# A banded attention with a three-way maximum feed-forward: one written-out order of work replaced by another

## The chip, the cores and the metric

The kernel runs on one core of a Trainium2 chip. The core has a matrix engine (TensorE, in the profile PE, with its weight loads as PEld), a vector engine (VectorE, DVE), a scalar engine (ScalarE, ACT), a general one (GpSimd, POOL) and a sync engine (SyncE, SP), which here issues nearly all transfers (DMAs). They run side by side and wait for each other by semaphores. Matmul results go to PSUM, 8 banks of 512 fp32 columns for 128 partitions; everything else lies in SBUF.

The metric is the device time of one execution in microseconds. The kernel before takes 175.69 us (median of 3 runs, 175.66 to 176.38).

## The reference

```
q, k, v: [4, 8, 768, 64] fp32          # batch, heads, positions, width
scores = q k^T / 8                     # per batch and head
keep   = (key < 8) or (0 <= query - key < 96)
bias   = -slope[head] * dist           # dist = query - key inside the band, 96 for a global key outside it
a      = softmax(where(keep, scores + bias, -1e9))
x      = (a v), heads side by side: [3072, 512]
h      = max(x w1, x w2, x w3)         # [3072, 768]
out    = h w_out                       # [3072, 512] fp32
```

## The kernel before, in words

The 3072 rows are 24 tiles of 128, six per batch. A query tile sees its own key tile and the one before it. The 8 global keys of a batch are kept from its first tile and copied over rows of later tiles that are no longer needed, so that "the tile before" also brings the global keys. Softmax needs no maximum: exp, a product with a mask that holds exp(bias) (or a bias that PE adds to the scores beforehand), a column of ones in v for the row sums, and a division at the end.

The feed-forward works on 7 chunks of 4, 2, 2, 4, 4, 4 and 4 tiles (`SIZES`). For each chunk c and each of 6 blocks f of the 768 columns, three groups of four matmuls (j = 0, 1, 2 for w1, w2, w3) go to three banks; the first is copied out, the second and third are merged by maxima.

Nothing is scheduled by a compiler. `SCHEDULE` is a string of some 780 units, and each engine works through its instructions in the order of the string. A unit may end in `@slot`, the place in a ring of buffers (`RINGS`) or the first PSUM bank that it takes, and a last digit may say which engine does it (0 ACT, 1 DVE, 2 POOL). T is a tile, G a pair of tiles, g a half of the heads, a is 0 for q, 1 for k, 2 for v.

| unit | work | line |
|---|---|---|
| l a.G.p | load q, k or v of a pair; p = 2 all heads, 0 or 1 a half. G = 12 loads q or k of the first four tiles, where p = 2, 3 are quarters | L229, L236 |
| c a.G.p.e | cast q or k to bf16; on POOL in two halves | L195, L201 |
| x, y | transpose on PE, copy out of PSUM | L270, L276; L283, L287 |
| X T | transposing DMA of a tile's q and k in place of x and y | L292 |
| v T.e.w | cast half of a tile's v | L254 |
| G T.w, V T.e.w | copies of the global keys, and of the global values | L313, L315; L323, L325 |
| B, K, R | bias rows, mask rows, their base | L373, L378, L561 to L565 |
| b, S T.g | bias by PE into the scores' bank; scores | L335, L349 |
| e T.g, m T.g | exp on ACT; product with the mask (left out where b was used) | L356; L365, L367 |
| A T, n T | attention product; division by the row sums | L391, L394; L402, L403 |
| t, u | x transposed by PE and copied out (ACT or DVE) | L418, L421 |
| Z T | x transposed by a DMA instead | L424 |
| w, W; q, Q | load and cast w1 to w3; load and cast w_out | L514, L195, L201; L523 |
| F c.f.j | four matmuls of the feed-forward | L433 |
| f c.f.j.w | j = 0: copy out (ACT or DVE); j = 1, 2: maximum (DVE) | L447; L449, L452 |
| O, o, s | output matmuls of a tile, copy out, store | L457, L471, L477 |
| E | output of the last chunk, with banks and staging slots from `LAST_BANKS` and `LAST_STAGES` | L457, L462, L463 |
| D n.w | n matmuls of w columns of zeros, which nothing reads | L532 |

In the body, the string is all that sets the order (the setup stands between the second and the third unit):

```
for u in todo[:2] + [None] + todo[2:]:
    ...
    code, _, slot = u.partition("@")
    units[code[0]](int(slot) if slot else None, *(int(n) for n in code[1:].split(".") if n))
```

Two rings matter below. PSUM's 8 banks are shared: a feed-forward group or an output takes one, scores and attention products take two, and a unit can start only when the unit that emptied its bank is done. Transfers of SP's queue are issued strictly in order, each behind its own waits: for its buffer, for the data it reads, and, after the first eight, for the landing of an earlier one.

Of the kernel before, what the change touches and what calls it, by code (L numbers as in the profile page):

```python
# [34 lines left out]
    F0.2.0@5 f0.4.0.1@1 F0.1.0@6 v4.1.2 v4.0.2 l2.3.2@0 f0.1.0.0@2 q2@0 v5.1.0 F0.0.0@0 F0.5.1@1 F0.4.1@4  # L35
    F0.2.1@6 m4.0.1 f0.0.0.0@3 v5.0.0 f0.5.0.0@4 m5.1.1 A4@2 V4.1.0 F0.3.1@0 W0.1.2 f0.4.1.1 W0.2.0 m5.0.1
    f0.5.1.1 F0.0.1@1 F0.1.1@4 V4.0.1 W1.2.0 n4@1 t4@7 A5@2 W2.2.0 c1.3.2.2@0 f0.0.1.1 f0.1.1.1 F0.1.2@1
    n5@0 u4.1@1 f0.1.2.1@0 F0.0.2@4 q0@1 t5@7 u5.0 q1@2 f0.3.1.1 f0.0.2.1 F0.2.2@2 F0.3.2@3 f0.3.2.1
    c0.3.2.0 f0.2.0.0@2 f0.2.1.1 F1.2.0@4 F1.0.2@7 Q2.0 v7.1.2 F1.0.0@5 f1.0.0.1@3 v6.1.2 F1.0.1@3 f0.2.2.1
    f1.0.1.1 f1.2.0.1@0 Q0.2 f1.0.2.1@1 x3.1.2@6 y3.1.2.1@3 F0.4.2@5 f0.4.2.1 l1.4.2@3 v6.0.2 Q1.2 F1.1.0@0  # L40
    F1.2.2@1 l0.4.2@4 l1.6.2@5 F1.2.1@4 f1.2.1.1 F1.3.1@2 f1.2.2.1 F1.3.2@3 v7.0.2 F1.3.0@4 f1.3.0.0@2
    f1.3.1.1 f1.3.2.1 x3.0.2@1 F0.5.2@5 f0.5.2.1 F1.4.0@2 F1.1.1@3 f1.1.0.0@3 y3.0.2.0 S6.0.0@0 S6.1.0@4
    G6.2 c1.4.2.2@1 c0.4.2.2 l0.5.2@0 c0.5.2.2@2 f1.1.1.1 f1.4.0.0@1 e6.0@4 S7.0.0@6 S7.1.0@2 l1.5.2@6
    c1.5.2.2 e6.1@5 c1.6.2.2@0 e7.1@6 F1.4.1@0 e7.0@7 l2.4.2@1 O0.2@1 f1.4.1.1 m7.1.1 x4.1.2@0 F1.5.2@2
    F1.5.0@3 m7.0.1 v8.1.2 F1.5.1@4 A7@6 f1.5.0.1@0 m6.1.1 m6.0.1 o0.2.0@0 y4.1.2.0@0 f1.5.1.1 f1.5.2.1
    x4.0.2@3 y4.0.2.0 G7.0 l0.6.2@1 c0.6.2.2 F1.4.2@5 O0.1@4 f1.4.2.1 n7@2 o0.1.1@1 A6@0 l2.5.2@2 S8.1.0@2
    S8.0.0@6 n6@3 V7.1.1 G8.1 v8.0.2 F1.1.2@4 O0.3@5 t6@0 v11.0.2 v9.0.2 v9.1.2 f1.1.2.1 V7.0.0 t7@1 e8.1@0
    e8.0@3 S9.0.0@2 u6.0@2 S9.1.0@6 m8.1.1 u7.1 o0.3.0@2 O0.0@4 e9.1@1 m8.0.1 o0.0.0@3 e9.0@2 F2.4.0@5
    m9.1.1 f2.4.0.0@2 A8@0 V8.0.2 n8@1 F2.5.0@4 F2.2.1@6 f2.5.0.1@4 F2.1.0@7 f2.1.0.0@0 G9.0 F2.5.1@5 V8.1.2
    F2.2.0@4 f2.5.1.1 m9.0.1 f2.2.0.0@1 X10@1 X11 S10.1.0@0 f2.2.1.1 e10.1@6 S10.0.0@2 e10.0@7 v10.0.1 X12@2  # L50
    G10.1 G12.1 F2.4.1@7 A9@4 V9.1.2 V9.0.2 X13 O1.0@6 l2.7.2@0 n9@0 S12.0.0@0 f2.4.1.1 m10.0.1 l2.6.2@1
    v10.1.1 e12.0@4 S11.1.0@2 S11.0.0@4 e11.1@5 F2.2.2@7 f2.2.2.1@0 F2.3.0@0 F2.1.1@1 F2.0.0@7 f2.3.0.0@3
    m10.1.1 e11.0@0 f2.0.0.0@1 A10@2 V10.0.2 f2.1.1.1 m11.1.1 o1.0.0@4 n10@3 Z8@0 V10.1.0 l0.7.2@2 v11.1.2
    v15.1.2 v12.1.2 F2.5.2@0 O1.1@1 v12.0.2 S12.1.0@2 e12.1@3 S13.1.0@4 m11.0.1 Z9 f2.5.2.1 S13.0.0@6
    o1.1.1@5 F2.4.2@0 A11@2 n11@2 F2.0.1@1 e13.1@1 F2.3.1@4 m12.0.1 m12.1.1 e13.0@2 c0.7.2.1@1 Z10 f2.0.1.1
    m13.1.1 F2.0.2@5 f2.3.1.1 t11@2 F2.1.2@3 l0.9.2@3 l1.8.2@4 u11.0 G13.0 f2.1.2.1 f2.0.2.1 F2.3.2@6
    F3.4.0@2 F3.0.0@1 f3.4.0.0@4 f3.0.0.1@0 m13.0.1 v13.1.1 f2.4.2.1 F3.1.0@4 F3.3.0@5 c0.9.2.0@2 f3.3.0.0@1
    A12@2 n12@1 f2.3.2.1 f3.1.0.1@2 F3.1.1@1 f3.1.1.1 v13.0.1 l1.9.2@0 c1.9.2.1 F3.0.2@0 F3.0.1@5 f3.0.1.1
    F3.1.2@4 f3.0.2.1@1 F3.2.0@1 F3.2.2@2 l1.7.2@6 c1.7.2.2 f3.1.2.1 F3.5.0@3 A13@4 V13.1.1 f3.5.0.1@3 n13@0
    l2.9.2@2 l0.8.2@5 c0.8.2.2@0 v19.0.2 V13.0.0 f3.2.0.0@0 v14.0.2 F3.5.1@0 l2.8.2@1 F3.2.1@6 f3.2.1.1  # L60
    f3.2.2.1 F3.3.1@1 F3.5.2@3 v18.1.0 X14@3 v14.1.2 X15 f3.5.1.1 f3.3.1.1 F3.4.1@2 c1.8.2.0 S14.0.0@4
    S14.1.0@0 e14.0@6 G14.2 f3.4.1.1 F3.4.2@6 f3.5.2.1 F3.3.2@7 e14.1@7 f3.4.2.1 m14.0.1 m14.1.1 v19.1.2
    v15.0.2 S15.0.0@0 e15.0@0 S15.1.0@2 G15.1 e15.1@5 f3.3.2.1 O2.0@6 A14@0 V14.1.2 o2.0.1@6 n14@3 X18@0
    O2.1@7 v18.0.0 o2.1.0@7 m15.0.1 S18.0.0@0 S18.1.0@2 X19 Z13@1 V14.0.1 O3.3@6 m15.1.1 e18.0@3 e18.1@4
    X16@1 o3.3.0@8 A15@0 n15@2 O3.0@7 S19.1.0@0 v17.1.1 m18.0.1 S16.1.0@2 m18.1.1 e19.1@1 S16.0.0@4 O3.2@6
    o3.0.1@9 e16.0@2 V15.1.2 A18@0 e16.1@6 n18@0 o3.2.1@10 m16.1.1 X17 O3.1@7 G16.0 Z14 o3.1.0@11 m16.0.1
    V15.0.1 S17.0.0@0 v16.0.0 Z12 S19.0.0@2 Z15 e19.0@7 S17.1.0@4 e17.1@0 m17.1.1 F4.4.0@6 e17.0@5 l0.11.2@1
    s1.0 l2.10.2@0 F4.2.0@7 l1.10.2@2 F4.1.0@2 F4.5.0@3 v16.1.0 F4.3.0@0 A16@4 f4.2.0.0@2 Z18@2 V16.1.2
    f4.3.0.0@0 v20.0.2 G18.0 F4.1.2@1 f4.1.0.1@3 c0.11.2.2@1 m17.0.1 v17.0.1 l2.11.2@2 n16@3 s3.1 f4.5.0.0@4
    V16.0.2 m19.0.1 l0.10.2@3 F4.0.1@0 F4.1.1@7 m19.1.1 f4.4.0.0@1 F4.5.2@6 c0.10.2.2@2 A19@2 Z16 n19@1 Z19  # L70
    G19.0 s0.1 V19.0.2 s2.1 f4.1.1.1 f4.1.2.1@0 V19.1.1 F4.0.0@4 F4.4.1@5 A17@2 c1.10.2.0 f4.0.0.1@3 n17@2
    F4.5.1@7 f4.5.1.1 F4.2.1@1 F4.3.2@4 f4.5.2.1 f4.4.1.1 F4.0.2@2 F4.3.1@3 F4.4.2@5 f4.2.1.1 v22.1.1
    f4.0.1.1 f4.3.1.1 f4.0.2.1 f4.3.2.1 F4.2.2@1 Z17 F5.1.1@0 F5.2.0@3 F5.5.0@2 s1.1 F5.3.0@4 F5.0.0@6
    f4.2.2.1 f5.3.0.0@4 f5.0.0.0@3 v21.1.2 F5.1.0@1 s0.0 l1.11.2@0 F5.3.1@4 c1.11.2.2 f5.2.0.1@0 f4.4.2.1
# [537 lines left out]
```

## Time and profile before

| | |
|---|---|
| median of 3 runs | 175.69 us (175.66 to 176.38) |
| the profiled execution | 176.69 us, of which the span of the trace is 174.8 us |
| TensorE clock granted | 0.996 of full speed |
| transfers | 37.36 MB, mean 214 GB/s |

The page gives busy times of the engines, the chain of work that ended last, and the costliest groups of instructions with a mean in ns and the idle time in front of them. Other views are the windows (busy time of each engine in a stretch, in the order PE, PEld, DVE, ACT, POOL, each with its count of instructions, then the granted clock, the share of the DMA engines that is busy, and GB/s), the chain in order of time (start, length, what), and the timeline (start, length, engine, line, operation, out<-in, count, and in brackets the idle time before it and what ended it). In the groups by form, the two numbers behind the bar are the busy time in us and the mean of one in ns.

### The profile page before, as it was taken

What the parts mean: (1) busy time and instruction counts of PE and PEld (TensorE: products, weight loads), DVE (VectorE), ACT (ScalarE), POOL (GpSimd) and SP (SyncE); (2) the same over time, 40 slices, a digit from 0 to 9 for tenths busy, and PEclk for the clock granted to TensorE, in tenths of its full rate; (3) what the DMA queues carried; (4) which work ended last, traced back from release to release, by engine and by line L of the source; (5) the groups of instructions that cost most, each with busy time, mean ns of one, the idle gap of its engine ahead of it and who ended that gap; (6) DMA issues with size and microseconds to landing.
All of it is one profiled execution on the core that took longest, in us unless ns stands there. A gap on an engine that the chain in (4) does not pass through costs nothing.

```text
span 174.8 us, 3865 instructions
## 1 busy us (share of the span) xinstructions
PE 165.9 (95%) x1485; PEld 93.6 (54%) x1507; DVE 131.9 (75%) x268; ACT 95.4 (55%) x147; POOL 54.7 (31%) x99
## 2 busy tenths in 40 slices
...
GB/s 149 352 292 327 402 360 385 270 371 311 229 303 179 139 183 266 267 290 284 165 135 112 114 145 306 305 210 260 231 213 20 0 120 137 121 286 4 0 119 185
DMA packets 66403, 37.36 MB, mean 214 GB/s; under 512 B 24144, under 2 KB 61392, under 8 KB 66384
## 3 DMA queue, kind: packets, MB, share of 16 engines
...
q8 instruction: 12, 0.20, 0.5%
q10 hardware_dynamic: 144, 0.07, 0.1%
...
## 4 chain that ended last, share of the span: by engine, by line
PE 76%; DVE 10%; DMA 6%; ACT 3%; issue 2%; SPq 0%; DVEq 0%
PE psum L433 44%; PE psum L457 17%; PE psum L349 6%; DMA xT<-xb 3%; DMA rawqk<-in_k_dram 3%; DVE P L365 3%; PE psum L391 3%; PE psum L394 2%; PE psum L276 2%; DVE ht L452 1%; DVE xb L403 1%; ACT P L356 1%; PE psum L270 1%; DVE qb L195 1%; PE psum L335 1%
## 5 line engine op out<-in xcount | busy, mean ns | idle before, releaser
L433 PE MATMUL psum<-xT,w 128*128 128x512 bf16 (+1 forms) x491 | 97.5, 348 | 1.5 <-DMA xT<-xb 0.7
L433 PEld LDWEIGHTS <-w 128*128 128x128 bf16 x504 | 47.6, 98 | 42.9 <-DMA xT<-xb 0.9
L356 ACT ACTIVATE P<-psum 128x1024 bf16<-128x1024 f32 (+1 forms) x48 | 43.3, 954 | 10.4 <-PE psum L349 10.3
L449 DVE TENSOR_TENSOR h<-h,psum 128x512 bf16<-128x512 bf16 (+1 forms) x42 | 25.0, 605 | 15.9 <-PE psum L433 12.4
L457 PE MATMUL psum<-wo,ht 128*128 128x512 bf16 (+2 forms) x147 | 33.4, 362 | 0.5
L447 ACT CAST h<-psum 128x512 bf16<-128x512 f32 (+1 forms) x27 | 13.8, 523 | 33.1 <-PE psum L433 29.8
L452 DVE TENSOR_TENSOR ht<-h,psum 128x512 bf16<-128x512 bf16 (+1 forms) x42 | 26.2, 644 | 2.1 <-PE psum L433 0.9
L365 DVE TENSOR_TENSOR P<-P,wmask 128x1024 bf16<-128x1024 bf16 x34 | 25.2, 752 | 2.0 <-ACT P L356 1.7
L457 PEld LDWEIGHTS <-ht 128*128 128x128 bf16 x156 | 13.8, 98 | 13.5 <-DVE ht L452 0.2
L254 POOL CAST va<-rawv 64x512 bf16<-64x512 f32 x28 | 18.5, 668 | 4.8 <-DMA rawv<-in_v_dram 3.7
L323 POOL COPY va<-vaf 4x260 int32<-4x260 int32 x17 | 7.2, 424 | 34.9 <-PE psum L394 34.5
L403 DVE TENSOR_TENSOR xb<-psum,rz 128x512 bf16<-128x512 f32 x24 | 16.6, 692 | 0.8
L201 POOL CAST qb<-rawk 128x512 bf16<-128x512 f32 x12 | 7.5, 654 | 23.7 <-DMA rawk<-in_k_dram 23.7
L349 PE MATMUL psum<-qkT 64*128 64x128 bf16 x352 | 14.4, 217 | 0.5 <-DVE qkT L315 0.4
L391 PEld LDWEIGHTS <-P 128*128 128x128 bf16 x192 | 12.6, 97 | 3.2 <-ACT P L356 0.4
L349 PEld LDWEIGHTS <-qkT 64*128 64x128 bf16 x352 | 10.0, 94 | 7.9 <-issue 5.9
L391 PE MATMUL psum<-va,P 128*128 128x65 bf16 x160 | 12.7, 193 | 0.7 <-DVE ht L452 0.6
L447 DVE CAST h<-psum 128x512 bf16<-128x512 f32 (+1 forms) x15 | 9.1, 615 | 5.1 <-PE psum L433 5.1
L471 ACT COPY staging<-psum 128x512 f32<-128x512 f32 x14 | 8.2, 592 | 8.8 <-PE psum L457 8.8
L201 POOL CAST qb<-rawq 128x512 bf16<-128x512 f32 x14 | 8.9, 664 | 9.0 <-DMA rawq<-in_q_dram 5.0
L394 PEld LDWEIGHTS <-P 128*128 128x128 bf16 x160 | 10.5, 97 | 2.1 <-issue 0.7
L394 PE MATMUL psum<-va,P 128*128 128x65 bf16 x128 | 9.9, 193 | 0.0
...
## 6 DMA issues: line engine op xcount, KB each, us to landing
...
```

Of the source, the lines that this page charges most:

```text
L254: copies[how](heads(va(T))[64 * e:64 * e + 64, :, 0:D], src)
L349: nc.tensor.matmul(sp[:, hh, j2, ds], qT(T - ds, 1, hsl, jp), qT(T, 0, hsl, jp), start=not how, stop=True, skip_group_check=True)
L356: nc.scalar.activation(P[:, :, 0:n], sps[T, g].rearrange("p a b d n -> p (a b) d n")[:, :, 0:n], AF.Exp, bias=0.0, scale=scale)
L365: mul(P, P, wmask[:, g, :, 0:2])
L391: nc.tensor.matmul(o, P[:, i, 0], heads(va(T))[:, h], start=True, stop=(t == 0), skip_group_check=True)
L394: nc.tensor.matmul(o, P[:, i, 1], heads(va(T - 1))[:, h], start=False, stop=True, skip_group_check=True)
L403: nc.vector.tensor_tensor(out=x.rearrange("p (g h) d -> p g h d", g=2), in0=o4[:, :, :, 0:64], in1=rz[:, :, :, None].to_broadcast([128, 2, ...
L433: nc.tensor.matmul(ps, w123[f // 2][:, j, dm, (f % 2) * 128:(f % 2) * 128 + 128], xT[c][:, dm], start=(dm == 0), stop=(dm == 3))
L447: copies[how](h01, ps)
L449: nc.vector.tensor_max(h01s[c, f], h01s[c, f], ps)
L452: nc.vector.tensor_max(dst, h01s[c, f].rearrange("p (t e i) -> p t e i", e=2, i=64), ps.rearrange("p (t e i) -> p t e i", e=2, i=64))
L457: nc.tensor.matmul(po, ht[c][:, f, tt * 128:(tt + 1) * 128], wo[:, f, cols], start=(f == 0), stop=(f == NF - 1))
```

## The change

The string `SCHEDULE`, `LAST_BANKS` and `LAST_STAGES` are replaced; `SIZES`, `RINGS` and all code are as before. The new string has 778 units in place of 782. In words: q and k of the first four tiles are loaded in whole halves of the heads instead of one half and two quarters each; the order of nearly all later units, their slots and the engines that do casts and copies are drawn up anew. The new order comes from a planner that laid it out under five draws of late transfers and in which copies of global keys wait while GpSimd is busy.

How often each engine has a unit (counted in both strings):

| unit | before ACT, DVE, POOL | after ACT, DVE, POOL |
|---|---|---|
| c | 4, 8, 14 | 5, 11, 8 |
| v | 6, 10, 32 | 16, 14, 18 |
| V | 4, 11, 17 | 10, 17, 5 |
| G | 9, 8, 3 | 7, 9, 4 |
| W | 4, 2, 3 | 3, 6, 0 |
| B | 1, 7, 0 | 2, 6, 0 |
| f, j = 0 | 27, 15, 0 | 22, 20, 0 |
| o | 14, 6, 0 | 13, 7, 0 |
| u | 6, 3, 0 | 7, 3, 0 |

Tile 9's Z9 has become t9 and u9, so 14 units Z stand against 15 and 10 units t against 9; there are three units D (D10.512, D4.256, D3.256) against two (D10.512, D3.256). The counts of F, O, S, e, m, b, A, n and X are the same.

```
 SCHEDULE = """
-    l0.12.1@0 l1.12.1@1 D10.512@0 l1.12.3@2 l0.12.2@3 l0.12.3@4 R K7 K6 B1.1 K4 B2.1 K2 B3.0 K1 K5 B0.1 B6.1
-    K0 c0.12.3.2@0 l1.12.2@5 c0.12.1.1 B4.1 B5.1 c1.12.1.1@1 K3 x12.0.1@0 y0.0.1.0@0 B7.1 l2.0.2@0 D3.256@1
...
-    e3.1@7 V2.1.2 n0@1 t0@2 W0.0.2 c1.2.2.1 u0.0@0 x2.1.2@3 y2.1.2.0@2 w1.2@2 x2.0.2@2 A3@4 t1@6 u1.0 n2@2
-    y2.0.2.1 t2@7 n3@3 l0.3.2@1 l1.3.2@2 S4.1.0@0 V3.1.2 e4.1@0 V3.0.2 S4.0.0@2 W1.1.2 u2.1 t3@6 G4.1 u3.0
-    W2.0.1 S5.1.0@4 e5.1@2 S5.0.0@0 e5.0@1 m4.1.1 W1.0.1 e4.0@3 F0.5.0@7 F0.4.0@6 W2.1.0 F0.3.0@4 f0.3.0.0@0
...
+    l0.12.1@0 l1.12.1@1 R B7.1 B5.1 l1.12.0@2 l0.12.0@3 B0.0 K6 B3.0 K1 B2.1 K7 B6.1 l2.0.2@0 D10.512@0
+    c0.12.1.1@0 x12.0.1@0 l2.1.2@1 c1.12.0.2@1 K0 B4.1 K5 B1.1 v1.1.2 v1.0.2 b0.0@2 y1.0.1.0@0 c1.12.1.1
+    x12.1.1@1 y0.1.1.0@1 K4 y0.0.1.1 y1.1.1.1 b0.1@4 D4.256@6 S1.1.0@6 l1.2.2@4 l0.2.2@5 v0.1.2 D3.256@0
+    x12.1.0@0 v0.0.2 S0.1.1 c0.12.0.1 e1.1@0 m1.1.1 v2.1.2 x12.0.0@1 y0.0.0.1 y1.0.0.1 e0.1@1 b1.0@6 b2.0@4
...
+    v3.0.1 A1@2 v3.1.1 e2.0@4 e2.1@5 G2.1 n1@0 b3.1@6 S3.1.1 b3.0@4 w0.0@0 w0.1@1 c0.2.2.2 A0@0 e3.1@6
+    V1.1.1 V1.0.1 S3.0.1 e3.0@7 A2@2 V2.1.2 x2.1.2@6 y2.1.2.0@2 t1@7 n0@1 t0@0 u0.0@0 x2.0.2@1 l2.2.2@2 n2@2
+    G3.2 t2@2 u2.0 V2.0.1 A3@4 y2.0.2.1 S4.0.0@0 S4.1.0@2 e4.0@0 n3@3 t3@6 G4.1 u1.1 W1.0.1 W2.0.1 w0.2@2
+    u3.0 S5.1.0@4 e5.1@3 W0.0.1 m5.1.1 K3 K2 e4.1@1 m4.1.1 m4.0.1 W0.1.1 v4.1.1 V3.0.0 S5.0.0@0 e5.0@2
+    V3.1.0 v4.0.1 F0.2.0@6 f0.2.0.0@0 F0.4.0@7 F0.3.0@4 w1.1@1 F0.0.0@5 F0.1.0@2 F0.5.0@3 F0.1.1@6
...
+    V10.1.1 m12.0.1 F2.5.1@6 e13.1@3 F2.0.1@7 v12.0.0 V10.0.1 f2.5.1.1 A11@4 Z8@0 F2.1.0@6 F2.5.2@0 F2.1.1@1
+    l1.7.2@0 f2.4.1.1 n11@3 v13.1.1 v13.0.1 t11@2 f2.1.0.1@2 F2.0.2@4 u11.1 F2.1.2@5 Z10 u9.0 F2.4.2@3
...
+    o2.1.1@10 m18.0.1 e19.1@7 A16@0 A18@2 G19.1 m19.0.1 n16@0 m19.1.1 V16.1.1 V16.0.1 Z15 F4.4.0@6 F4.3.0@4
+    n18@1 F4.2.1@5 s1.1 s3.1 A19@0 f4.3.0.1@3 A17@2 l0.10.2@6 n19@2 l1.10.2@0 o3.0.0@11 F4.1.1@4 n17@3
+    V19.0.1 c1.10.2.1@0 c0.10.2.1 l1.11.2@1 F4.1.0@7 f4.1.0.1@4 F4.0.0@0 F4.2.0@1 c1.11.2.1@2 f4.2.0.1@2
+    f4.4.0.1@1 f4.0.0.1@0 f4.2.1.1 V19.1.1 l2.11.2@2 F4.3.1@2 f4.1.1.1 f4.3.1.1 F4.4.2@3 v23.0.1 F4.0.2@1
...
-LAST_BANKS = (6, 7, 3, 0, 1, 4, 5, 2)
+LAST_BANKS = (4, 5, 6, 7, 1, 0, 3, 2)
-LAST_STAGES = (8, 2, 0, 10, 11, 7, 6, 3, 4, 9, 1, 5)
+LAST_STAGES = (11, 1, 10, 5, 8, 9, 2, 4, 6, 0, 3, 7)
```

104 lines of the change are left out of this document (47 added, 57 removed).

## The prediction

> **What bounds the kernel now.** I read the page's busy table first, then a table of windows, then the chain that ended last.
>
> ```profile
> span 174.8 us, 3865 instructions
> PE 165.9 (95%) x1485; PEld 93.6 (54%) x1507; DVE 131.9 (75%) x268; ACT 95.4 (55%) x147; POOL 54.7 (31%) x99
> ```
>
> TensorE (PE) is busy for 165.9 of 174.8 us. Of the 8.9 us that are left, 3.6 us are the tail after its last matmul (below: the last copy starts at 171.19). A plan that only reorders work can therefore win some 5 us at the very most. The windows say where those microseconds lie:
>
> ```profile
> 10.00:15.00 5.00, 4.29 (x70) 2.35 (x67) 4.70 (x10) 4.63 (x8) 3.25 (x6) 1.00 1.20 290
> 15.00:20.00 5.00, 4.69 (x90) 3.55 (x90) 4.34 (x10) 4.07 (x6) 3.37 (x6) 1.00 1.08 376
> 70.00:75.00 5.00, 4.29 (x32) 2.67 (x32) 4.23 (x11) 2.58 (x5) 0.00 (x0) 1.00 1.07 270
> 80.00:85.00 5.00, 4.41 (x35) 2.33 (x35) 4.18 (x7) 1.17 (x3) 3.03 (x5) 1.00 1.13 249
> 110.00:115.00 5.00, 4.83 (x50) 2.73 (x50) 4.29 (x9) 0.62 (x1) 1.03 (x2) 1.00 1.44 284
> ```
>
> PE (the first busy column) idles 1.0 us in 10 to 20, 0.7 in 70 to 75, 0.6 in 80 to 85 and 0.2 in 110 to 115; elsewhere it runs on. In these windows DVE (third) is the fullest engine beside it, and in the first two ACT is as full. The chain names what held PE there:
>
> ```profile
> 21.58 0.38 PE psum L433
> 67.78 4.98 DMA xT<-xb
> 79.97 1.13 DVE qb L195
> 108.28 2.79 DVE P L365 x2
> 155.42 9.23 PE psum L433 x42
> 171.19 0.58 ACT staging L471
> ```
>
> So: chunk 0 of the feed-forward starts at 21.6; a transposing transfer (tile 10, unit Z10) ends the wait before chunk 3; a DVE cast is on the chain near 80; two DVE mask products are on it near 108; the end is PE. The fifth row also gives PE's pace, 0.22 us per 512-column matmul, 0.88 per feed-forward group of four.
>
> **What the change moves between engines.** Counting the units of both orders: of the v casts (L254) 14 leave POOL, 10 to ACT and 4 to DVE; of the copies of global values (L323, L325) 12 leave POOL, 6 to ACT and 6 to DVE; 6 whole query/key casts and one quarter leave POOL; all 3 weight casts leave it. Five evacuations of a first product go from ACT to DVE. Their prices:
>
> ```profile
> L254 POOL CAST va<-rawv 64x512 bf16<-64x512 f32 x28 | 18.5, 668 | 4.8 <-DMA rawv<-in_v_dram 3.7
> L254 DVE CAST va<-rawv 64x512 bf16<-64x512 f32 x8 | 3.4, 423 | 0.1
> L254 ACT CAST va<-rawv 64x512 bf16<-64x512 f32 x4 | 2.5, 618 | 0.0
> L323 POOL COPY va<-vaf 4x260 int32<-4x260 int32 x17 | 7.2, 424 | 34.9 <-PE psum L394 34.5
> L325 DVE COPY va<-vaf 4x520 bf16<-4x520 bf16 x11 | 4.2, 381 | 0.9 <-PE psum L394 0.8
> L325 ACT COPY va<-vaf 4x520 bf16<-4x520 bf16 x4 | 2.5, 621 | 7.9 <-PE psum L394 7.9
> L201 POOL CAST qb<-rawk 128x512 bf16<-128x512 f32 x12 | 7.5, 654 | 23.7 <-DMA rawk<-in_k_dram 23.7
> L201 POOL CAST w<-staging 128x512 bf16<-128x512 f32 x6 | 5.0, 858 | 3.2 <-DMA staging<-in_moe_w_dram 3.2
> L195 DVE CAST w<-staging 128x1024 bf16<-128x1024 f32 x2 | 1.4, 686 | 0.0
> L447 DVE CAST h<-psum 128x512 bf16<-128x512 f32 x11 | 7.5, 686 | 4.9 <-PE psum L433 4.8
> L447 ACT CAST h<-psum 128x512 bf16<-128x512 f32 x19 | 10.9, 585 | 28.1 <-PE psum L433 24.8 <-DVE ht L452 3.1
> L365 DVE TENSOR_TENSOR P<-P,wmask 128x1024 bf16<-128x1024 bf16 x34 | 25.2, 752 | 2.0 <-ACT P L356 1.7
> ```
>
> POOL loses 14 x 0.668 + 12 x 0.424 + 12 half casts x 0.654 + 6 half casts x 0.858, about 27 us, half of its work. DVE gains 4 x 0.423 + 6 x 0.381 + 4 x 0.686 (weights) + 5 x 0.686 (evacuations) + about 2 for three query/key casts, some 12 us, to 144 (83% of the span). ACT gains 10 x 0.618 + 6 x 0.621, less 5 x 0.585, some 7 us, to 102. From the moment chunk 2 starts until late in chunk 5 POOL has nothing left.
>
> **PE's own work** (+0.3). The order of the built program has 8 more matmuls: four dummies of 256 columns (D4) and the four transposes of tile 9, which now goes through PE instead of a transposing transfer.
>
> ```profile
> L532 PE MATMUL psum<-zeros 128*128 128x256 bf16 x3 | 0.5, 273 | 0.0
> L418 PE MATMUL psum<-identb,xb 128*128 128x128 bf16 x36 | 3.2, 220 | 0.0
> ```
>
> The dummies cost 4 x 0.5/3 = 0.7 but stand at 8 us, where PE waits for the first exponential and the value casts anyway: nothing on the path (0.7 if that cover were gone). The transposes cost 4 x 3.2/36 = 0.35: on the path, 0.3.
>
> **Whole first loads and the start** (+0.3). Bytes to the same point are the same: both orders bring 2 MB of q and k and then v. Four quarter casts become one DVE cast and one POOL cast of a half. These end later, but behind them stands POOL, which now does more in a row:
>
> ```profile
> 11.18 1.37 POOL L254 CAST va<-rawv 64x512 bf16<-64x512 f32 x2 [1.91 <-DMA rawv<-in_v_dram]
> 16.12 1.63 POOL L201 CAST qb<-rawq 128x512 bf16<-128x512 f32 x2
> 17.33 1.20 PE L276 MATMUL psum<-identb,qb 128*128 128x128 bf16 x16 [0.25 <-DVE qb L195]
> 18.64 0.69 DVE L287 COPY qkT<-psum 128x1024 bf16<-128x1024 bf16 x1 [0.53 <-PE psum L276]
> 20.03 1.02 ACT L356 ACTIVATE P<-psum 128x1024 bf16<-128x1024 f32 x1
> 20.95 0.58 ACT L421 COPY xT<-psum 128x512 bf16<-128x512 bf16 x1
> 21.42 2.88 ACT L356 ACTIVATE P<-psum 128x1024 bf16<-128x1024 f32 x3
> 8.63 0.40 PE L349 MATMUL psum<-qkT 64*128 64x128 bf16 x8
> ```
>
> The first values land at 11.18 (fifth load in the new order, seventh in the old, the same 2.5 MB). Then POOL casts v for tiles 1, 0 and 2: 6 x 0.668 = 4.0, to 15.2; the first attention product A1 needs the first four, at 13.9 instead of 13.1. Then k and q of tiles 2 and 3, both on POOL now (k was DVE's): 2 x 1.63, to 18.5. From there to chunk 0: transposes 0.6, copy on DVE 0.69, scores 0.4, exponential of tile 4 1.02, copy of tile 3 (unit u3, queued behind that exponential on ACT) 0.58: 21.8 or 21.9 instead of 21.6. Bounds: -0.5, if POOL keeps its best pace of 0.61 for each v and the casts are done a microsecond sooner; +1.3, if the 0.8 by which A1 is late adds up with it. I take +0.3.
>
> **First stretch of chunk 0** (+0.3). After u3 ACT has, in its order, three exponentials (2.88), two mask rows K3 and K2 (moved here from the setup; 0.44 each by the row below) and two copies V3 (0.62 each), 5.0 in all, before the first evacuation f(0,2,0); that one takes 0.585 and frees bank 6. PE issues six groups in the meantime, 6 x 0.88 = 5.3 at most, and the seventh (F0.1.1) wants bank 6. So 21.85 + 5.0 + 0.6 = 27.4 against 27.1: a wait of 0.3. In the order of before both mask rows stood in the setup and both copies on POOL.
>
> ```profile
> 3.50 1.76 ACT L378 ACTIVATE wmask<-rbase 128x384 bf16<-128x384 f32 x4 [1.27 <-DVE rbase L565]
> ```
>
> **What comes back in the middle** (-1.4). At 72.8 PE waited for Z10, issued at 67.8 because tile 10's normalisation was late on DVE. In the new order tile 9 needs no transfer and Z10 stands behind one load less; A10 stands 41 us of PE work behind the start of chunk 0, which with 2 us for short waits like those of before puts it at 65; with its normalisation (0.9), the wait in SP's queue (1) and the 5 us of the row above to land, Z10 is there near 72, and chunk 3 starts near 74. That gives back the 0.7 of window 70 to 75. Near 80 and 108 DVE was slow while POOL was at work:
>
> ```profile
> 108.19 2.86 DVE L365 TENSOR_TENSOR P<-P,wmask 128x1024 bf16<-128x1024 bf16 x2
> 14.44 0.53 DVE L315 COPY qkT<-kg 128x32 bf16<-128x32 bf16 x1
> L315 DVE COPY qkT<-kg 128x32 bf16<-128x32 bf16 x6 | 1.6, 275 | 0.0
> ```
>
> Two mask products took 2.86 where two take 1.5 by their mean, and the cast at 79.97 took 1.13 where 0.69 is usual. With POOL empty in chunks 2 to 4 these go: 0.6 of window 80 to 85 and 0.2 of 110 to 115, less what structure keeps. I take -1.4 of 1.5; bounds 0 and -1.5.
>
> The Trainium skill, "SBUF — State Buffer", section "Who interferes with whom", says that DVE copies and casts in a two-port mode, and DVE operations with two SBUF inputs, share a port pair with GpSimd under an exclusive lock: whichever started first holds it for its whole instruction. The long products and the 0.53 us copy agree with it. By the rule the change also pays at the start, where POOL runs without a gap from 11.2 to 18.9 and DVE has seven such copies; that is the fourth case below, and by the rule alone the sum would be that case's.
>
> **New waits** (+0.7). From tile 17's masks to the second groups of chunk 4 DVE has four products (0.752), one output copy and three maxima (each taken as an evacuation, 0.686), four normalisations (0.692 and a short reciprocal, together 0.9), three casts (0.686) and five evacuations, some 15 us. PE has four attention products (16 matmuls of 65 columns, by its pace 0.03 each, so 0.5) and eight groups, 9 us.
>
> ```profile
> L403 DVE TENSOR_TENSOR xb<-psum,rz 128x512 bf16<-128x512 f32 x24 | 16.6, 692 | 0.8
> ```
>  Eight banks let DVE fall behind by about six groups, 5 us, so I find PE fed, but with margins of some 0.3 us at each bank. ACT is as tight at tiles 15 to 19: seven long and two short exponentials, five v casts and copies and three output copies, some 13 us in a stretch of 13. I found margins from 0.1 to 0.7 in both places. The trace of before shows no such stretch; its bounds are 0 (all margins hold) and +3 (DVE's 15 us plus its own waits replace PE's). Nearest is the row of 80 to 85, where a full DVE cost 0.6; I take 0.7.
>
> **Sum.** +0.3 (tile 9) + 0.3 (start) + 0.3 (bank 6) - 1.4 + 0.7 = +0.2 us. The profiled execution spans 174.8 and took 176.69 in all; the median of the runs is 175.69, 0.9 above that span. Expected: span 175.0, median 175.9. A change under 0.5% (0.88 us) is about what the measurement can't tell from none.
>
> **Rivals.**
> - *Faster: the start costs nothing and the room holds.* POOL's casts at their best pace and a bank 6 that is free in time remove both +0.3, the margins hold (no +0.7), and the -1.4 stays with tile 9's +0.3: 174.8 - 1.1, median 174.6. For it: DVE's stalls on the chain near 80 and 108 are with POOL, which is gone there. Against it: DVE at 83%.
> - *Slower: DVE becomes the bound around tiles 16 to 19.* Once DVE is behind by more than the six free banks (5 us), each of its microseconds is PE's. It starts even, gains 15 - 9 = 6 us there, so 1 us is over at once, and each wait inside it adds. I price it at +2: 177.9. For it: ACT does nearly nothing in chunk 4, so all evacuations are DVE's. Against it: these operations overlap by nearly 0.1 each, which would make 15 us 13.5.
> - *The transfers stay late.* The queue is 1.07 to 1.20 full in the windows above, so Z10 may again arrive after PE is ready. The 0.7 is not won: 176.6.
> - *POOL's run at the start slows DVE.* Seven small copies and casts each lose about 0.3, as the 0.53 against 0.275 shows, 2 us on DVE, of which half reaches tile 3: +1.0, 176.9.
>
> **Chances.** Forecast 0.34, with its own range 175.0 to 176.7; faster 0.23; DVE bound 0.20; late transfers 0.13; start 0.10. Leaving out about one in ten at each end gives 174.2 to 178.1. Faster by over 0.5% (below 174.8): 0.25, the second case and a little of the first. Slower (above 176.57): DVE's 0.20, half of the late transfers, most of the start, a little of the first: 0.35. Same: 0.40.
>
> **What would show it.** Right: POOL busy near 27, DVE near 144; chunk 0 starting near 21.9 with a short wait before its seventh group; no PE wait on a transfer before chunk 3; PE over 4.7 in each 5 us of 70 to 85; no mask product above 0.8 us after chunk 2. Wrong: chunk 0 before 21 or after 23; DVE busy without gaps and PE below 4.5 of 5 from 95 to 115; a cast of q or k on DVE that waits for its load, with evacuations queued behind it, in chunk 4.

## The result and the profile after

The changed kernel takes 176.99 us (median of 13 runs, 176.59 to 177.43) against 175.72 us (175.25 to 176.42, 13 runs) for the kernel before on the same chip: a ratio of 1.0063, 95% interval [1.0049, 1.0078]. The forecast was 175.9, from 174.2 to 178.1: the time lies inside, 1.1 us above the point, and 0.3 above the 175.0 to 176.7 that the forecast's own case had. The profiled execution spans 175.7 us, against 174.8. Both profiled executions are longer than their kernels' medians (177.43 us against 176.99, and 176.69 against 175.72), so the spans differ by 0.9 where the medians differ by 1.27. What follows explains the difference of the two traces; the remaining 0.4 stays open.

The page's busy table, and the table of windows after:

```profile
span 175.7 us, 3860 instructions
PE 165.7 (94%) x1495; PEld 93.8 (53%) x1515; DVE 142.0 (81%) x291; ACT 102.2 (58%) x157; POOL 30.0 (17%) x56
```
```profile
15.00:20.00 5.00, 4.29 (x87) 3.60 (x86) 4.68 (x9) 3.79 (x6) 3.38 (x7) 1.00 1.08 372
70.00:75.00 5.00, 4.95 (x56) 4.02 (x56) 3.49 (x9) 3.48 (x7) 0.00 (x0) 1.00 1.20 141
80.00:85.00 5.00, 4.95 (x44) 2.65 (x44) 4.77 (x12) 2.59 (x5) 0.00 (x0) 1.00 1.20 292
90.00:95.00 5.00, 4.95 (x50) 2.61 (x50) 4.75 (x10) 4.89 (x8) 0.00 (x0) 1.00 0.89 161
95.00:100.00 5.00, 4.75 (x52) 2.54 (x52) 4.72 (x13) 4.95 (x8) 0.00 (x0) 1.00 1.24 209
```

The busy times came out as worked out beforehand: POOL 30.0 (27 foretold), DVE 142.0 (144), ACT 102.2 (102). PE is nearly without a gap where it had waited (4.95 in 70 to 75 and in 80 to 85), but at 15 to 20 it has 4.29 instead of 4.69, and from 90 to 100 ACT is full (4.89 and 4.95 of 5) with PE at 4.75. Longer windows make the balance; first the kernel before, then the changed one:

```profile
40.00:60.00 20.00, 19.83 (x232) 14.85 (x233) 16.11 (x34) 14.00 (x23) 14.49 (x25) 1.00 1.06 235
70.00:90.00 20.00, 18.54 (x129) 9.63 (x131) 17.92 (x35) 7.94 (x12) 5.80 (x10) 1.00 1.10 235
90.00:110.00 20.00, 19.84 (x198) 10.43 (x200) 15.81 (x30) 15.32 (x25) 3.54 (x8) 1.00 0.81 170
```
```profile
40.00:60.00 20.00, 19.28 (x234) 14.55 (x235) 18.01 (x36) 15.87 (x26) 15.22 (x23) 1.00 1.12 265
70.00:90.00 20.00, 19.84 (x170) 11.36 (x172) 17.09 (x36) 14.97 (x24) 0.00 (x0) 1.00 1.28 223
90.00:110.00 20.00, 19.36 (x208) 10.57 (x211) 18.76 (x44) 13.86 (x20) 0.00 (x0) 1.00 1.03 216
```

PE wins 1.30 us between 70 and 90, and loses 0.55 between 40 and 60 and 0.48 between 90 and 110. The rest of the loss stands before chunk 0.

The windows can't be added up to the end, since the two orders have done different work at the same time. So I take the start of each chunk's first matmul from the trace and add the PE work that its order has still to do, counted in units at one pace for both kernels (a feed-forward group of four 0.856, the others in proportion). This is the end in sight; where it rises from one chunk to the next, PE was idle or slower than this pace. Single steps of the table are therefore rough: over chunk 2 of the changed kernel the end rises by 1.02, though PE is busy for 9.95 of the 10 us from 60 to 70 and for 4.95 of the next 5.

| end in sight at the start of | chunk 0 | 1 | 2 | 3 | 4 | 5 | 6 | last output |
|---|---|---|---|---|---|---|---|---|
| before | 167.36 | 167.39 | 168.27 | 169.68 | 171.00 | 171.17 | 171.88 | 172.01 |
| after | 168.31 | 168.41 | 169.65 | 170.67 | 172.11 | 172.05 | 172.72 | 172.86 |
| later by | 0.95 | 1.02 | 1.38 | 0.99 | 1.11 | 0.88 | 0.84 | 0.85 |

By this table the start costs 0.95, of which 0.2 is tile 9's work on PE and 0.74 a later chunk 0 (22.17 instead of 21.43 us, by its first weight load); chunks 0 and 1 cost 0.43; chunks 2 to 4 give back only 0.50; the rest changes nothing.

What holds PE at the start stands in the timelines of DVE, POOL and PE of the changed kernel:

```profile
15.74 1.61 DVE L325 COPY va<-vaf 4x520 bf16<-4x520 bf16 x2
15.38 1.17 POOL L201 CAST qb<-rawk 128x512 bf16<-128x512 f32 x2
16.60 1.23 POOL L201 CAST qb<-rawq 128x512 bf16<-128x512 f32 x2
17.41 0.19 PE L394 MATMUL psum<-va,P 128*128 128x65 bf16 x1 [0.71 <-DVE va L325]
17.86 0.61 PE L276 MATMUL psum<-identb,qb 128*128 128x128 bf16 x8
```

POOL casts k of tiles 2 and 3 from 15.38 to 16.55 and q from 16.60 to 17.83, sooner than expected. But beside them DVE takes 1.61 us for two copies of global values (V1), which elsewhere take 0.3 each. Tile 2's attention product (A2) waits 0.71 for them, and k's transposes, behind A2 in PE's queue, begin at 17.86, 1.3 us after k was cast. In chunk 1 the same shows:

```profile
48.02 1.63 POOL L201 CAST qb<-rawq 128x512 bf16<-128x512 f32 x2
48.07 1.10 DVE L365 TENSOR_TENSOR P<-P,wmask 128x1024 bf16<-128x1024 bf16 x1
49.56 0.60 PE L433 MATMUL psum<-xT,w 128*128 128x256 bf16 x4 [0.37 <-DVE h L449]
```

A mask product of 0.69 takes 1.10 beside POOL's cast (the one before it, over half as many columns, takes 0.78 instead of 0.42); the maximum behind them frees a bank late, and PE waits 0.37.

### The profile page after: what moved, and what is told of

The parts are those of the page before. It is cut to its first block, busy times and chain, and to the rows that moved or that the text cites. A ratio compares the mean times of both kernels' runs of the same rounds, so it can differ in the third digit from the quotient of the medians.

```text
span 175.7 us, 3860 instructions
## 1 busy us (share of the span) xinstructions
PE 165.7 (94%) x1495; PEld 93.8 (53%) x1515; DVE 142.0 (81%) x291; ACT 102.2 (58%) x157; POOL 30.0 (17%) x56
## 4 chain that ended last, share of the span: by engine, by line
PE 57%; DMA 16%; ACT 9%; DVE 6%; issue 5%; SPq 3%; POOL 2%; POOLq 0%; ACTq 0%; DVEq 0%
PE psum L433 37%; PE psum L457 11%; ACT P L356 5%; DMA rawv<-in_v_dram 5%; DMA rawqq<-in_q_dram 4%; DMA staging<-in_moe_w_out_dram 4%; PE psum L349 3%; DMA qkT<-qb 3%; PE psum L391 2%; PE psum L394 2%; POOL va L254 1%; DVE P L365 1%; DVE w L195 1%; SPq L236 1%; DVE va L325 1%
## 5 line engine op out<-in xcount | busy, mean ns | idle before, releaser
L447 ACT CAST h<-psum 128x512 bf16<-128x512 f32 (+1 forms) x22 | 10.9, 510 | 46.0 <-PE psum L433 45.7
L452 DVE TENSOR_TENSOR ht<-h,psum 128x512 bf16<-128x512 bf16 (+1 forms) x42 | 26.1, 644 | 1.7 <-PE psum L433 0.8
L365 DVE TENSOR_TENSOR P<-P,wmask 128x1024 bf16<-128x1024 bf16 x35 | 24.4, 714 | 2.4 <-ACT P L356 1.9
L403 DVE TENSOR_TENSOR xb<-psum,rz 128x512 bf16<-128x512 f32 x24 | 16.6, 692 | 0.8
L447 DVE CAST h<-psum 128x512 bf16<-128x512 f32 (+1 forms) x20 | 12.2, 625 | 2.8 <-PE psum L433 2.8
L315 POOL COPY qkT<-kg 128x32 bf16<-128x32 bf16 x3 | 0.6, 209 | 69.1 <-PE psum L349 69.0
L471 ACT COPY staging<-psum 128x512 f32<-128x512 f32 x13 | 7.4, 589 | 8.3 <-PE psum L457 8.3
L254 POOL CAST va<-rawv 64x512 bf16<-64x512 f32 x16 | 11.0, 689 | 3.2 <-DMA rawv<-in_v_dram 2.4
L254 ACT CAST va<-rawv 64x512 bf16<-64x512 f32 x14 | 8.7, 618 | 0.2
L201 POOL CAST qb<-rawq 128x512 bf16<-128x512 f32 x8 | 5.2, 675 | 17.9 <-DMA rawq<-in_q_dram 17.7
```

Source lines behind the costliest of these rows:

```text
L254: copies[how](heads(va(T))[64 * e:64 * e + 64, :, 0:D], src)
L365: mul(P, P, wmask[:, g, :, 0:2])
L403: nc.vector.tensor_tensor(out=x.rearrange("p (g h) d -> p g h d", g=2), in0=o4[:, :, :, 0:64], in1=rz[:, :, :, None].to_broadcast([128, 2, ...
L447: copies[how](h01, ps)
L452: nc.vector.tensor_max(dst, h01s[c, f].rearrange("p (t e i) -> p t e i", e=2, i=64), ps.rearrange("p (t e i) -> p t e i", e=2, i=64))
```

## The experiments

Each kernel was timed twelve times (the first six, the second five times) beside the kernel before on the same chip; ratios are to that. A change of 0.25% (0.4 us) is about what such a pair of intervals tells apart.

**1 and 2. The two orders joined at chunk 0.** One kernel goes by the old order up to the start of chunk 0 and by the new one after it, the other the other way round.

```
-<changed order up to its first unit F>
+<order of before up to its first unit F> m5.1.1 m4.0.1 W0.1.1 v4.1.1 v4.0.1
 <rest of the changed order, less what is done already>
```
```
-<order of before up to its first unit F>
+<changed order up to its first unit F> w1.1 w1.2 l0.3 l1.3 W1.1.2
 <rest of the order of before, less what is done already>
```

> The order up to chunk 0 is that of before (quarter loads, its engines and slots), all behind it is the new order. Theory 'start': nearly the whole loss arises before chunk 0 (chunk 0 starts at 22.2 instead of 21.4, and one transposed tile and the dummies are added), the rest of the new order is as fast as the old: chunk 0 at 21.4 to 21.6, span 174.8 to 175.0, 0 to +0.2% on before. Theory 'rest': the loss arises behind the start, in chunk 1 (+0.4) and at tiles 15 to 19 (+0.4): still +0.4% to +0.7%.

> The mirror of the run before: the new order up to chunk 0, behind it the order of before. Theory 'start': chunk 0 at 22.1 and the loss of the change, +0.4% to +0.7%. Theory 'rest': within 0.2% of before, since a late start is taken up by the wait for tile 10's transfer before chunk 3.

Measured: old start, new rest 177.98 us, ratio 1.0127 [1.0088, 1.0166]; new start, old rest 178.62 us, 1.0151 [1.0127, 1.0174]. Both are slower than either parent. The PE rows of the first and of the second kernel say why:

```profile
22.58 5.35 PE L433 MATMUL psum<-xT,w 128*128 128x512 bf16 x23 [0.95 <-ACT P L356]
```
```profile
28.32 4.48 PE L433 MATMUL psum<-xT,w 128*128 128x512 bf16 x20 [1.93 <-DVE h L447]
```

The joints make waits of their own of 1 to 2 us: banks and weights that one order has ready in time for its own chunk 0 come late for the other's. These two runs don't divide the loss into a start and a rest; an order is not the sum of its halves. The next ones change single units.

**3. The cast of k at the start on DVE.**

```
-... S2.1.1 c1.2.2.2@2 e1.0@3 ... w0.1@1 c0.2.2.2 A0@0 e3.1@6 V1.1.1 V1.0.1 S3.0.1 ...
+... S2.1.1 e1.0@3 ... w0.1@1 A0@0 e3.1@6 V1.1.1 V1.0.1 c1.2.2.1@2 c0.2.2.2 S3.0.1 ...
```

> The new order with one cast moved: k of tiles 2 and 3 (c1.2.2) goes from POOL to DVE, behind the copies V1.1 and V1.0. In the changed kernel these two copies took 1.61 us, beside that cast on POOL, and PE waited 0.7 us for them before A2. Theory 'GpSimd holds the copies': with POOL idle there the pair takes 0.6, the wait before A2 goes, chunk 0 starts at 21.4 to 21.7 and the span is 0.5 to 0.7 shorter than 175.7. Theory 'length of POOL's run': the copies stay at 1.6 because another POOL instruction stands beside them; chunk 0 starts earlier by at most 0.3.

Measured: 176.57 us, 1.0035 [1.0014, 1.0056]. DVE and POOL there:

```profile
15.76 0.60 DVE L325 COPY va<-vaf 4x520 bf16<-4x520 bf16 x2
16.29 0.68 DVE L195 CAST qb<-rawk 128x1024 bf16<-128x1024 f32 x1
16.69 1.31 POOL L201 CAST qb<-rawq 128x512 bf16<-128x512 f32 x2 [1.23 <-DMA rawq<-in_q_dram]
17.03 0.62 PE L276 MATMUL psum<-identb,qb 128*128 128x128 bf16 x8
```

The pair of copies takes 0.60 instead of 1.61 with POOL idle beside it, A2's wait is gone, k's transposes begin at 17.03 instead of 17.86, and chunk 0 starts at 21.69 instead of 22.17, although DVE now has a cast more. At the last output the end in sight is 0.91 sooner (171.95 against 172.86); the other 0.4 arises between the starts of chunks 3 and 4, where the edit changes nothing. The ratio is 0.3% lower than the changed order's, about what the intervals can tell apart.

So in this pair of executions DVE's copies beside POOL's cast are worth about 0.5 us. But it is not a fixed price. Runs 6 and 7 below leave k on POOL as the changed kernel does, and there the same two copies took 1.07 and 1.10; here they are in run 6:

```profile
15.64 1.29 POOL L201 CAST qb<-rawk 128x512 bf16<-128x512 f32 x2
16.00 1.07 DVE L325 COPY va<-vaf 4x520 bf16<-4x520 bf16 x2
```

Counted from POOL's first cast of v, chunk 0 starts after 10.33 and 10.35 us in runs 6 and 7, as in run 3 (21.69 - 11.34 = 10.35); the changed kernel needs 10.86 (22.17 - 11.31) and the kernel before 10.25 (21.43 - 11.18). So the short collision costs PE no more than the cast that run 3 gives to DVE, and run 3's gain is against the long one, 1.61, alone (run 2 has that too). Of the 0.74 by which chunk 0 came later, the long collision is 0.51, a later first v 0.13, and the order itself 0.10.

**4. Four casts of the middle from POOL to ACT, in the order of before.**

```
-c1.7.2.2 ... c0.8.2.2@0 v19.0.2 V13.0.0 f3.2.0.0@0 ... c0.11.2.2@1 ... v20.0.2
+c1.7.2.0 ... c0.8.2.0@0 v19.0.2 V13.0.0 f3.2.0.0@0 ... c0.11.2.0@1 ... v20.0.0
```

> The kernel before with four casts taken from POOL to ACT, which is nearly idle there: c1.7.2, c0.8.2, c0.11.2 and v20.0. Tests the relief alone. Theory 'GpSimd slows DVE': the two mask products near 108 take 1.4 instead of 2.86, the cast near 80 takes 0.7 instead of 1.13, the windows 80 to 85 and 110 to 115 win up to 0.8 together: -0.2% to -0.5%. Rival: the slow DVE is hidden by waits that stay (transfers): within 0.15%.

Measured: 177.05 us, 1.0053 [1.003, 1.0076]: slower. In DVE's timeline, the cast of 1.13 us of before is one of 0.69 now, and the two mask products near 108 take 1.28 instead of 2.86, so GpSimd did slow DVE there; but ACT and PE show a new wait:

```profile
79.61 0.69 DVE L195 CAST qb<-rawk 128x1024 bf16<-128x1024 f32 x1
108.56 1.28 DVE L365 TENSOR_TENSOR P<-P,wmask 128x1024 bf16<-128x1024 bf16 x2
```
```profile
83.73 1.04 ACT L195 CAST qb<-rawq 128x1024 bf16<-128x1024 f32 x1 [2.62 <-DMA rawq<-in_q_dram]
85.83 2.75 PE L433 MATMUL psum<-xT,w 128*128 128x512 bf16 x12 [1.14 <-ACT h L447]
```

The cast waits 2.62 us for its load at the head of ACT's queue; behind it stand a copy and the evacuation that frees PE's bank, and PE waits 1.14. POOL was the engine on which that wait for a load cost nothing.

**5. A maximum ahead of two mask products in chunk 1**, on top of run 3.

```
-... x4.1.2@0 m6.1.1 m7.0.1 f1.2.1.1 f1.4.2.1 l0.5.2@4 ...
+... x4.1.2@0 f1.2.1.1 f1.4.2.1 m6.1.1 m7.0.1 l0.5.2@4 ...
```

> The changed order with k of tiles 2 and 3 cast by DVE as in the third run, and with the maxima f1.2.1.1 and f1.4.2.1 put ahead of the two mask products m6.1.1 and m7.0.1 on DVE in chunk 1. Theory A (the 0.37 to 0.48 us that PE waits near 49.5 for bank 1 comes from DVE, whose products of 0.78 and 1.10 us beside GpSimd's casts hold back the maximum): with the maximum first, the wait before O0.2 is gone, and tile 7's attention product does not wait instead, because the masks have 3 us until it. Chunk 2 starts 0.4 to 0.5 us sooner than in the third run (58.14), and the time is 0.3 to 0.5 us below the third run's, 1.000 to 1.002 of the kernel before on the same chip. Theory B (that stretch is bound by the chain of the v transfer, POOL's casts and ACT's exponentials up to chunk 2): the wait reappears before S10 or F2.3.0, and the time equals the third run's, 1.0035.

Measured: 177.18 us, 1.0057 [1.0037, 1.0078]: no gain. The wait moved on by one bank, behind the next maximum of DVE, which now stands behind the long products:

```profile
49.02 1.09 DVE L365 TENSOR_TENSOR P<-P,wmask 128x1024 bf16<-128x1024 bf16 x1
50.98 0.93 PE L349 MATMUL psum<-qkT 64*128 64x128 bf16 x16 [0.37 <-DVE ht L452]
```

Theory A fell as far as the order on DVE goes: it is DVE's lost time, not the place of one maximum, that PE meets.

**6. Four v casts of tiles 17 and 19 from ACT to POOL**, in the changed order.

```
-v19.0.0 ... v17.0.0 ... v17.1.0 ... v19.1.0
+v19.0.2 ... v17.0.2 ... v17.1.2 ... v19.1.2
```

> The changed order with four v casts of tiles 17 and 19 given from ACT to GpSimd, which is empty there. Theory A (the new waits at tiles 15 to 19, 0.53 before O3.2 at 95 and 0.37 before S19 at 101, come from ACT's load of 2.5 us of v casts): both waits go, the projected end gains 0.4 to 0.9 us between 90 and 105, and the ratio to the kernel before is about 1.003 instead of 1.006. Theory B (GpSimd's casts hold DVE where they lie beside its copies and products): the mask products of tiles 15 to 17 rise from 0.69 to 0.9 or more and DVE, which has only small gaps there, passes the loss on; the gain is 0.2 or less, or a loss, and the ratio stays at 1.006 or above.

Measured: 176.40 us, 1.0015 [0.999, 1.004], 0.5% better than the changed order. The profiled execution is 1.3 us longer in span than the median of the timed ones; it shows the new margin as well as the new risk. First, from the changed kernel, PE's scores of tile 16, a wait for ACT, the last scores of tile 18, and the scores of tile 19:

```profile
93.38 0.62 PE L349 MATMUL psum<-qkT 64*128 64x128 bf16 x16
95.60 0.19 PE L391 MATMUL psum<-va,P 128*128 128x65 bf16 x1 [0.20 <-ACT P L356]
100.84 0.28 PE L349 MATMUL psum<-qkT 64*128 64x128 bf16 x4
101.36 0.62 PE L349 MATMUL psum<-qkT 64*128 64x128 bf16 x16 [0.23 <-DMA qkT<-qb]
```

Then, from this run, the three groups of scores, which PE does in the same order, and POOL and DVE there:

```profile
92.72 0.62 PE L349 MATMUL psum<-qkT 64*128 64x128 bf16 x16
99.82 0.29 PE L349 MATMUL psum<-qkT 64*128 64x128 bf16 x4
101.60 0.62 PE L349 MATMUL psum<-qkT 64*128 64x128 bf16 x16 [1.50 <-DMA qkT<-qb]
90.14 2.40 POOL L254 CAST va<-rawv 64x512 bf16<-64x512 f32 x4 [30.99 <-DMA rawv<-in_v_dram]
90.19 0.73 DVE L452 TENSOR_TENSOR ht<-h,psum 128x512 bf16<-128x512 bf16 x1
91.04 0.69 DVE L403 TENSOR_TENSOR xb<-psum,rz 128x512 bf16<-128x512 f32 x1
93.18 1.29 DVE L365 TENSOR_TENSOR P<-P,wmask 128x1024 bf16<-128x1024 bf16 x2
```

From tile 16's scores to the last of tile 18 PE takes 7.46 us in the changed kernel and 7.46 or 7.47 in runs 1, 3, 5 and 7, which also have the four casts on ACT and all show a wait for ACT of 0.19 or 0.20. It takes 7.10 here and 7.09 or 7.10 in runs 9 to 12, which have the casts on POOL and no such wait. So 0.36 of the loss there was ACT's load: theory A, a little below its 0.4 to 0.9. Then this execution waits 1.50 for tile 19's transposing transfer, for which the changed kernel waited 0.23: it lets PE go on at 101.60 here and at 101.36 there, so what PE had gained was lost again. Theory B was not tested: while POOL casts, DVE's operations read PSUM (L452, L403) and take their usual time, POOL takes its best, 0.60 a cast, and the mask products come after it.

**7. Quarters again**, in the changed order.

```
-l1.12.0@2 l0.12.0@3 ... c1.12.0.2@1 ... x12.1.0@0 ... c0.12.0.1 ... x12.0.0@1
+l1.12.2@2 l1.12.3@5 l0.12.2@3 l0.12.3@4 ... c1.12.2.2@1 c1.12.3.2 ... x12.1.2@0 x12.1.3 ... c0.12.2.1 c0.12.3.1 ... x12.0.2@1 x12.0.3
```

> The changed order with q and k of the second half of the heads of tiles 0 to 3 loaded and cast in quarters again, each cast by the engine that cast the half (k on GpSimd, q on DVE), all else as in the changed order but for the slots of two later loads. Theory A (whole loads cost nothing by themselves; the start is late through GpSimd's and DVE's queue): chunk 0 starts within 0.2 us of the changed kernel's 22.17 and the ratio stays near 1.006. Theory B (whole loads are the cost: their casts start later): chunk 0 starts 0.3 to 0.6 sooner and the ratio falls to 1.003. Against B and below A: each load more is one more issue on SP's queue, and the v of tiles 0 to 3 come behind two more, which could make the start up to 0.5 later.

Measured: 177.08 us, 1.005 [1.0025, 1.0076], between the two theories and not to be told from either by the intervals. In its one profile chunk 0 starts at 21.75, as theory B has it, but not through the loads: the v casts on POOL begin at 11.40 (11.31 in the changed kernel), and the pair V1 takes 1.10 instead of 1.61. Run 6, with whole loads and 1.07 for the pair, starts chunk 0 as soon after POOL's first cast of v (10.33 against 10.35 us). So the traces show no cost of whole loads, and the times don't exclude a small one.

```profile
15.84 1.10 DVE L325 COPY va<-vaf 4x520 bf16<-4x520 bf16 x2
```

**8. Tile 9 through PE and one cast of k from POOL to ACT**, in the order of before.

```
-... c1.7.2.2 ... Z9 ... t11@2 F2.1.2@3 ... u11.0 G13.0 ...
+... c1.7.2.0 ... t11@2 t9@6 F2.1.2@3 ... u11.0 u9.0 G13.0 ...
```

> The order of before with two edits: tile 9's transposing transfer replaced by transposes on PE, and the cast of k of tiles 14 and 15 (units c1.7.2) moved from GpSimd to ACT, which is idle there. Theory A (the two waits of the middle, 0.9 before chunk 3 for tile 10's transfer and 0.7 near 82 behind the DVE cast of 1.13 us, are worth what the prediction put on them): tile 9's transposes cost 0.25, the wait before chunk 3 falls from 0.9 to 0.3 or less because tile 10's transfer has one less ahead of it, the DVE cast near 80 takes 0.69 and the wait near 82 falls to about 0.25; together 0.6 to 0.9 us, a ratio of 0.995 to 0.997. Theory B (the waits are displaced: whatever PE gains before it meets again as a wait for the exponentials and masks of tiles 14 to 19 or a transfer that still lands near 72.8): the same or up to 0.3 us slower, 1.000 to 1.002.

Measured: 176.55 us, 1.0025 [1.0005, 1.0044]: theory B, no gain in time, although PE's busy time between 70 and 90 rises. Its windows and PE's row before chunk 3:

```profile
40.00:60.00 20.00, 19.48 (x229) 14.38 (x228) 16.30 (x34) 13.62 (x21) 15.10 (x26) 1.00 1.10 250
70.00:90.00 20.00, 19.18 (x148) 10.26 (x145) 17.59 (x34) 9.41 (x14) 4.01 (x8) 1.00 1.08 228
73.05 4.05 PE L433 MATMUL psum<-xT,w 128*128 128x256 bf16 x20 [0.50 <-ACT xT L421]
```

The wait before chunk 3 is now for the copy of tile 9's transposes, which I had put behind tile 11's on ACT, not for a transfer; and this execution lost 0.35 between 40 and 60, where the edits change nothing. So this run doesn't say what tile 10's transfer alone is worth. It shows that two of the changed order's ideas, set into the old order one by one, don't carry their gain over.

**9. Runs 3 and 6 together.**

```
-c1.2.2.2@2 ... c0.2.2.2 ... V1.1.1 V1.0.1 ... v19.0.0 ... v17.0.0 ... v17.1.0 ... v19.1.0
+V1.1.1 V1.0.1 c1.2.2.1@2 c0.2.2.2 ... v19.0.2 ... v17.0.2 ... v17.1.2 ... v19.1.2
```

> The changed order with two edits that each helped alone: k of tiles 2 and 3 cast by DVE (third run, 0.3% better than the changed order) and four v casts of tiles 17 and 19 on GpSimd (sixth run, 0.45% better). Theory A (the two costs are separate, one at the start, one at tiles 15 to 19, and PE is the end): they add up, ratio 0.998 to 1.000 to the kernel before, level with it or a little better. Theory B (PE that comes earlier meets transfers, as in the sixth run's profile, where it waited 1.5 us for tile 19's q and k): only one of the two is seen, 1.001 to 1.004.

Measured: median 176.02 us against 176.03 for the kernel before (35 runs); the ratio, pulled up by three runs of 0.8, 1.4 and 1.9 us above the median, is 1.0023 [0.9997, 1.0048]. By the medians the two edits recover the whole loss; by the ratio they are no better than run 6 alone. Whether they add up stays open. Against the changed order (1.0063) the ratio is 0.4% lower, which is more than the intervals leave to chance (0.3%). In this profile PE takes 7.09 us from tile 16's scores to the last of tile 18, as in run 6.

**10. POOL's queue in chunk 1 turned round**, on run 9.

```
-G6.2 f1.2.0.0@2 q2@2 Q0.2 v7.1.2 ... c1.5.2.2@2 m7.1.1 c0.5.2.2 ... v9.0.2 e8.0@1 G8.0 v8.0.2 V7.1.0
+f1.2.0.0@2 q2@2 Q0.2 v7.1.2 G6.2 ... c1.5.2.2@2 m7.1.1 ... v9.0.2 e8.0@1 G8.0 v8.0.2 c0.5.2.2 V7.1.0
```

> The kernel of the ninth run with GpSimd's queue in chunk 1 turned round: the copy of tile 6's global keys, for which GpSimd waited 2.25 us, goes behind two casts that were ready, and the cast of q of tiles 10 and 11 goes behind the v casts of tiles 8 and 9, so that GpSimd is idle from about 45.5 to 49 while DVE does the mask products of tiles 6 and 7. Theory A (GpSimd's casts slow DVE there, 0.78 and 1.10 us where 0.43 and 0.69 are usual, and PE's wait before O0.2 follows): the products take 0.43 and 0.69, the wait of 0.48 goes, chunk 2 starts 0.4 to 0.5 sooner, and the ratio is 0.002 to 0.003 below the ninth run's. Theory B (PE waits there for the chain of v of tiles 8 and 9 and for ACT): the products are short, but the wait moves to the next bank as in the fifth run, and the ratio is the ninth's.

Measured: 176.36 us, 1.0025 [0.9999, 1.0051], as run 9. POOL is idle beside the second product, which takes 0.68, and PE has no wait up to 58.8:

```profile
45.57 1.69 POOL L201 CAST qb<-rawk 128x512 bf16<-128x512 f32 x2 [1.23 <-DMA rawk<-in_k_dram]
47.46 0.68 DVE L365 TENSOR_TENSOR P<-P,wmask 128x1024 bf16<-128x1024 bf16 x1
49.08 2.30 POOL L254 CAST va<-rawv 64x512 bf16<-64x512 f32 x3 [1.82 <-DMA rawv<-in_v_dram]
```

But run 9's profile had no wait there either: its cast of q started 0.2 us after the product, which took 0.68, and was itself the slower one (1.52 for its two halves, 1.36 in run 10). In both, the end in sight rises by 0.7 to 0.9 over chunk 1 instead of 1.24. The profiles with PE's order of the changed kernel in chunk 1 show a pattern: where both masks are held up (0.66 to 0.78 and 1.09 or 1.10: the changed kernel, runs 1, 3 and 7) PE takes 19.51 to 19.57 us from the start of chunk 1 to that of chunk 2; where only one of them clearly is, or neither (runs 6 and 9 to 12), it takes 18.98 to 19.31. So POOL's casts cost the changed kernel's execution 0.2 to 0.5 us in chunk 1. The times of run 10 don't show it, because run 9 hadn't this loss either in its profile.

**11. Without the dummies D4**, on run 9.

```
-y1.1.1.1 b0.1@4 D4.256@6 S1.1.0@6
+y1.1.1.1 b0.1@4 S1.1.0@6
```

> The kernel of the ninth run without the four dummy matmuls at 8 us (D4). The prediction held them free, because PE waits there anyway. Theory A (free): chunk 0 starts at the same time within 0.1 us and the ratio is the ninth run's. Theory B (they stand on the path, since PE is never far ahead there): chunk 0 starts 0.2 to 0.5 us sooner and the ratio falls by 0.001 to 0.003. A third case, that PE's clock falls without them, would show as a granted clock below 1.0 and longer matmuls in the first 20 us.

Measured: 176.07 us, 1.0012 [0.9991, 1.0032]; PE's next scores start at 8.37 instead of 8.39, now after a wait, at a granted clock of 1.00. Free, as forecast:

```profile
8.37 0.40 PE L349 MATMUL psum<-qkT 64*128 64x128 bf16 x8 [0.46 <-ACT qkT L283]
```

**12. Tile 9 by a transfer again**, on run 9.

```
-... t9@3 ... Z8@0 ... Z10 u9.0 ...
+... Z8@0 Z9 ... Z10 ...
```

> The kernel of the ninth run with tile 9 transposed by a transfer again, as in the order of before, in SP's queue between those of tile 8 and tile 10. Theory A (the transfer of tile 10 sets the start of chunk 3, and PE's transposes of tile 9 pay for themselves by keeping the queue clear): PE saves 0.25 but waits before chunk 3 for tile 9 or 10, 0.5 to 1.0 us, so the ratio rises by 0.002 to 0.004 over the ninth run's. Theory B (PE comes to chunk 3 later than the transfer anyway, so it is hidden): no wait, and the ratio falls by 0.001 to 0.002.

Measured: 176.59 us, 1.0025 [1.0008, 1.0042]. Its profile has no wait before chunk 3, and its span is 0.2 us shorter than run 9's (174.1 against 174.3; 15.06 against 15.17 us from the start of chunk 2 to that of chunk 3), as theory B says; the median of its times is 0.57 longer, as A says; the ratio is nearly equal. It stays open whether tile 9's place matters.

## Why the prediction was right, and where it was not

The time is inside the range, and of the three outcomes it fell into "slower" by a little (0.63%), which had a chance of 0.35 against 0.40 for "same". That it lies inside is owed to the wide range. The sum of +0.2 stands against +0.85 by the end in sight, and +1.27 by the medians:

- **PE's own work** (+0.3). Right: the dummies are free (run 11), tile 9's transposes are the 0.2 of work left.
- **Whole loads and the start** (+0.3). The traces show no cost of the loads (runs 6 and 7). The start is mis-sized, 0.74 instead of 0.3, and by the wrong chain: I followed POOL's casts to 18.5 us, and they were done at 17.83. What was late was A2, behind V1's copies on DVE, and k's transposes behind A2. That is the fourth rival, "POOL's run at the start slows DVE", which I gave a tenth: run 3 shows its mechanism, at 0.5 instead of the 1.0 that I priced, and runs 6 and 7 show that a shorter collision costs nothing against run 3. That the rival's 176.9 us comes next to the 176.99 measured is luck, since only about half of its price came from its mechanism. The Trainium skill, "SBUF — State Buffer", "Who interferes with whom", has the rule (copies and casts of DVE in its two-port modes and GpSimd's work lock each other out of a shared port pair); the trace agrees with 1.61 beside 0.60. I had averaged over seven DVE operations where I should have asked which of them PE's next unit waits for.
- **Bank 6** (+0.3). Came, at half the size. ACT was through its exponentials, mask rows and copies 4.7 us after u3 (22.19 to 26.92) where I had 5.0, because its instructions overlap by some 0.1 each. The first evacuation then takes 0.58 and frees bank 6 at 27.50. At 0.215 a matmul PE would begin its seventh group at 27.41; it begins at 27.55, 0.14 later. The first row below, seven groups with one record missing, shows no gap, because the records of matmuls overlap; the second matmul row, which begins with the seventh group, and the weight loads show it:

```profile
22.24 6.34 PE L433 MATMUL psum<-xT,w 128*128 128x512 bf16 x27
26.92 0.58 ACT L447 CAST h<-psum 128x512 bf16<-128x512 f32 x1
27.55 0.81 PE L433 MATMUL psum<-xT,w 128*128 128x512 bf16 x3
27.56 0.53 PEld L433 LDWEIGHTS <-w 128*128 128x128 bf16 x3 [0.26 <-issue]
```

  Runs 3, 6, 7 and 9 have the same step of 0.14. The end in sight rises by 0.10 over chunk 0 (0.03 before).
- **Missed: chunk 1** (0 foretold, +0.36). I looked for slowed DVE operations only where they went away. In chunk 1 POOL casts k and q of tiles 10 and 11 while DVE does the masks of tiles 6 and 7. The profiles bear it out (run 10); times don't.
- **The middle** (-1.4). Nearly right: PE wins 1.30 between 70 and 90, the wait for tile 10's transfer does not appear, and the mask products are all at their best (from the view of one line, minimum, median and maximum in ns, from the start of chunk 2 on):

```profile
L365 DVE TENSOR_TENSOR P<-P,wmask x25: 666/684/694, 60.2 to 138.6; 128x1024 bf16<-128x1024 bf16 x25
```

  But in this execution the transfer was not sooner: it was issued at 67.6 and landed at 73.6, against 67.8 and 72.8 before. PE came to chunk 3 a microsecond later, at 73.80, and so didn't wait. In runs 3, 5 to 7 and 9 to 11, with the same order there, it landed between 70.7 and 72.6, at least 0.8 us before PE began chunk 3; in run 1 it landed at 74.48, just as PE began it (74.52). So the wait is gone in all of them, and the margin changes from one execution to the next.
- **New waits** (+0.7). Right in place and kind, 0.48 in size between 90 and 110. Run 6 and the runs that it is set beside name the engine: ACT, not DVE, with 0.36. The changed kernel loses another 0.41 behind it to tile 19's transfer (3.09 us from tile 18's last scores to chunk 4); runs 1, 3, 5 and 7, with the same order there, don't (2.68). The second rival, DVE as the bound around tiles 16 to 19, did not come: DVE is at 4.72 of 5 between 95 and 100, but PE's 0.36 came back with ACT's relief alone.

By the table the net of the last two is -0.5 where I had -0.7; the start and chunk 1 make up the rest of the difference.
